# Weight narrowing with a mask made one piece ahead, combinations split where they are formed, and block sums accumulated in PSUM

## The chip, the core and the metric

The kernel runs on one core of one Trainium2 chip. The metric is the device time of one execution in microseconds (us). TensorE multiplies matrices into PSUM (eight banks of 2 KB per partition), VectorE, ScalarE and GpSimd work element by element, and SyncE issues most of the DMAs from one queue, in order. Every engine works through its own instructions in order; a wait holds up all that stands behind it.

## The reference, cut to what matters

```python
def _attn_ref(q, k, v, w_pre, w_post):            # batch 4, 12 heads, 448 tokens, 64
    scores = scale * np.matmul(q, k.transpose(0, 1, 3, 2))
    scores = np.einsum('bhij,hg->bgij', scores, w_pre)
    attn = softmax(scores)                        # written out in the original
    attn = np.einsum('bhij,hg->bgij', attn, w_post)
    return np.matmul(attn, v)
...
def _moe_ref(x, w_in, w_out, g_ln):               # 1792 x 768, inner width 1024
    h = x @ w_in
    solu = h * softmax(h)
    ln = (solu - mu) / np.sqrt(var + 1e-06) * g_ln
    return ln @ w_out
...
def _moe2_ref(x, w_in, w_out):                    # inner width 2048
    r = np.maximum(x @ w_in, 0.0)
    return (r * r) @ w_out
```

All weights of the two MLPs are float64 in DRAM, read as pairs of 32-bit words. The matrices are float32; each product is made of three matmuls of operands that are split into a high part and a remainder ("hi" and "lo").

## The kernel before

**Stages.** Attention, then the first MLP over 14 tiles of 128 tokens, then the second MLP in sixteen rounds. The order on each engine is the order of the code; nothing reorders it.

**Narrowing.** A float64 weight becomes a float32 by bit operations on its two words. `narrow` (line 75) takes a piece of 128x256: a Square on ScalarE of the high word read as a float32 (to see where the exponent is too small), then line 83 (shift the high word, mask it), line 87 (add the sign and top bit) and line 91 (add three bits of the low word) on VectorE. Values that are too small are then set to zero: by `flush` (lines 100 and 101) on GpSimd in the first MLP, by one more VectorE pass (line 96) in the second. The weights of the second MLP are 96 pieces, narrowed by the generator `w2stream`, of which the other code takes a step now and then (`steps2`). It holds three raw pieces (`nraw`), one `nsq` and two results (`nt`); SyncE loads the raw ones and stores the results to DRAM (w2iD, w2oD). About two thirds of the pieces fall into the first MLP, the rest into rounds 0 to 6.

**First MLP.** For tile m: `h1` (36 matmuls of 512 columns, line 459); the first part of `norm1` (maximum at line 712, exp at 715, the product at 718, bn_stats, and on GpSimd the power that gives rs); five steps of narrowing; `zt(m-1)` (eight transposes, line 747, with a cast on ScalarE and a subtraction on VectorE); the rest of the norm (nb at line 729 on VectorE, the scaling at 732 on ScalarE); five steps; the split of a later tile of x; and from tile 4 on two groups of `out1` (24 matmuls each, line 761, whose result ScalarE copies at line 769 into a tile that is stored to x2D), with seven steps behind each.

**Hand-over.** `prepare` runs beside the last nine output groups. The second MLP uses seven products (p1 to p7) instead of eight block products, so x and the weights are combined first. `mix_x` loads the four blocks of x (xb), combines them with four subtractions on VectorE (lines 890 to 894) and stores the results to DRAM (xtD); `load_xc` reads operands back (xr); `split_xc` (lines 925 and 926) splits them on ScalarE and VectorE. `mix_w` and `split_ti` do the same for weights, on GpSimd (lines 964 and 980) and ScalarE (line 979).

**Second MLP.** A round q takes 256 of the inner columns for half of the tokens (rounds 0 to 7, then 8 to 15). The list SEQ gives TensorE's order: the seven products (`prod`, nine matmuls of 448 columns each, line 1050) and, between them, seven output tiles of the round before (`y2`, twelve matmuls of 384 columns, line 1119, added on VectorE at line 1130). p1 and p2 share a bank, as do p5 and p3, and p7 and p4. `after` (line 1074) takes the sums off: u = p1 + p6, then u + p5, u + p5 + p7, u + p5 + p3 and u + p7 + p4, with a copy on ScalarE (line 1080) and five additions on VectorE (lines 1082 to 1096); `square` follows on ScalarE, and `lows` gives the remainder on VectorE (line 1063).

## Time and profile before

| | |
|---|---|
| time, median of 3 runs | 1254.18 us (1250.58 to 1259.58) |
| the profiled execution | 1259.37 us, of which the span of its instructions is 1257.6 us |
| busy in the span | TensorE 1083.1 us (86%), VectorE 738.3 (59%), GpSimd 699.9 (56%), ScalarE 585.0 (47%) |
| mean granted clock of TensorE | 0.940 of full speed |
| attention | 0 to 406 us |
| first MLP with the hand-over | 406 to 762.6 us |
| second MLP | 762.6 to 1257.6 us |

A busy share is an average over stages; what a stage is bound by is read from a stretch of its own. Times inside the span are us from its start. In a row of a timeline the engine's idle time ahead of the instruction stands in brackets, with what ended it. PE is TensorE, PEld its weight load, DVE VectorE, ACT ScalarE, POOL GpSimd, SPq the queue of SyncE.

### The profile page before, as it was taken

The page shows a single profiled execution, that of the slowest core. Times are in us where ns is not written, and L with a number is a line of the kernel's source. Part 1 is how long each engine was busy: PE and PEld are TensorE (multiplying, and loading weights), DVE is VectorE, ACT ScalarE, POOL GpSimd, SP SyncE. Part 2 cuts the span into 40 slices and gives each one's busy share as a digit, 9 for nine tenths or more (in the row PEclk, how much of TensorE's full clock was granted, in tenths as well). Part 3 has the DMA queues.
Part 4 walks back from the last instruction along what each step waited for, and adds up shares of the span by engine and source line. Part 5 has one row for each costly group of instructions (what it writes and reads, how often), then busy time and mean ns, then how long its engine had stood idle before and what let it go on. Part 6 is the DMA issues. An engine that isn't in the chain of part 4 may idle for free.

```text
span 1257.6 us, 31153 instructions
## 1 busy us (share of the span) xinstructions
PE 1083.1 (86%) x12488; PEld 908.4 (72%) x12488; DVE 738.3 (59%) x1293; ACT 585.0 (47%) x1212; POOL 699.9 (56%) x910
## 2 busy tenths in 40 slices
PE   8898979889898855898798666998889999999998
PEld 3555656556667644687687666888778899999998
DVE  3557768658662644555556455778877563344444
ACT  4666666668663322332332224643434556444432
POOL 3657988877755554453554353556654655555531
PEclk9899999989998977898999787999989999999999
DMA  6777887777664433343343485454443352222102
GB/s 178 207 219 221 236 249 219 234 219 209 203 194 121 147 105 112 114 143 97 115 142 107 141 289 163 125 175 142 143 142 106 117 179 99 66 73 63 51 26 88
DMA packets 131936, 187.91 MB, mean 149 GB/s; under 512 B 24752, under 2 KB 104368, under 8 KB 131792
## 3 DMA queue, kind: packets, MB, share of 16 engines
q1 hardware_dynamic: 122948, 161.40, 41.7%
q0 software_dynamic: 6464, 22.60, 6.6%
q10 hardware_dynamic: 2380, 1.93, 0.6%
q8 instruction: 98, 1.61, 0.6%
q14 instruction: 46, 0.38, 0.1%
HBM read 106.45 MB, written 40.89 MB: 117 GB/s over the span
## 4 chain that ended last, share of the span: by engine, by line
PE 20%; DVE 16%; DMA 11%; issue 7%; POOL 6%; ACT 5%; SPq 1%; POOLq 0%; DVEq 0%; ACTq 0%
PE ps_y L1119 11%; PE ps_h L1050 9%; DMA w2iD<-nt 3%; DVE nt L87 2%; POOL nt L101 2%; DMA w2oD<-nt 2%; POOL nsq L100 2%; DMA xr<-x2D 2%; DVE nt L91 2%; DVE y L1130 2%; DMA xr<-xtD 1%; DVE st L721 1%; DVE e L718 1%; DMA w1oraw<-w1oD 1%; DVE nt L83 1%
## 5 line engine op out<-in xcount | busy, mean ns | idle before, releaser
L1119 PE MATMUL ps_y<-to,gt 128*128 128x384 f32 x1332 | 250.9, 342 | 17.5 <-DVE y L1130 17.2
L1119 PEld LDWEIGHTS ps_y<-to,gt 128*128 128x128 f32 x1332 | 238.8, 192 | 24.0 <-DVE y L1130 18.2
L1050 PE MATMUL ps_h<-xc,ti 128*128 128x448 f32 x1008 | 222.4, 373 | 17.1 <-DVE h L1085 10.7
L1050 PEld LDWEIGHTS ps_h<-xc,ti 128*128 128x128 f32 x1008 | 192.0, 192 | 34.9 <-ACT ti L979 11.0
L761 PE MATMUL ps_o<-zt,w1o 128*128 128x384 f32 (+1 forms) x720 | 136.1, 351 | 30.7 <-ACT o L769 27.9
L761 PEld LDWEIGHTS ps_o<-zt,w1o 128*128 128x128 f32 x720 | 130.2, 209 | 35.3 <-ACT o L769 31.7
L299 PEld LDWEIGHTS ps_ring<-w,e 60*64 60x64 f32 (+1 forms) x5760 | 103.3, 138 | 72.1 <-issue 41.1
L318 DVE COPY at<-ps_ring 128x420 f32<-128x420 f32 x156 | 87.8, 610 | 108.5 <-PE ps_ring L299 108.4
L299 PE MATMUL ps_ring<-w,e 60*64 60x60 f32 (+2 forms) x5760 | 112.2, 222 | 31.8 <-issue 23.8
L80 ACT ACTIVATE nsq<-nraw 128x256 f32<-128x256 f32 x96 | 41.7, 434 | 210.0 <-POOL nt L101 145.6
L215 ACT COPY ssrc<-ps_ring 128x896 f32<-128x896 f32 x92 | 82.3, 906 | 107.3 <-PE ps_ring L208 94.0
L459 PE MATMUL ps_h<-w1i,xs 128*128 128x512 f32 x504 | 126.1, 409 | 3.8 <-POOL xs L702 3.4
L1130 DVE TENSOR_TENSOR y<-ps_y,y 128x768 f32<-128x768 f32 x97 | 92.1, 952 | 50.2 <-PE ps_y L1119 50.2
L260 ACT ACTIVATE e<-ps_pre,nm 128x448 f32<-128x448 f32 x180 | 113.1, 639 | 13.7 <-DVE nm L253 10.8
L459 PEld LDWEIGHTS ps_h<-w1i,xs 128*128 128x128 f32 x504 | 97.9, 196 | 27.7 <-POOL xs L702 4.3
L980 POOL TENSOR_TENSOR ti<-s,ti 128x384 fp32r<-128x384 f32 x64 | 69.6, 1099 | 74.1 <-ACT ti L979 72.5
L253 DVE TENSOR_REDUCE nm<-ps_pre 128x1 f32<-128x448 f32 x180 | 103.2, 611 | 12.4 <-PE ps_pre L242 12.4
L208 PE MATMUL ps_ring<-k,q 64*64 64x448 f32 x752 | 100.7, 558 | 5.6 <-ACT ssrc L215 3.7
L242 PE MATMUL ps_pre<-sdst,wpre_bd 64*64 64x448 f32 x720 | 100.5, 570 | 4.4 <-issue 2.7
L1063 DVE TENSOR_TENSOR gt<-h,gt 128x448 fp32r<-128x448 f32 x64 | 48.7, 761 | 92.0 <-ACT gt L1068 90.4
L338 PEld LDWEIGHTS ps_ring<-at,v 128*64 128x64 f32 x1536 | 77.7, 142 | 31.0 <-PE ps_pre L242 12.0
L83 DVE TENSOR_SCALAR nt<-nraw 128x256 uint32<-128x256 uint32 x96 | 39.3, 409 | 94.0 <-DMA w2iD<-nt 53.8
(112 smaller groups left out, 1660.0 us busy)
## 6 DMA issues: line engine op xcount, KB each, us to landing
sdst<-ssrc SPq DMA_DIRECT2D x166, 210.0 KB
nraw<-in_moe_w_in_dram SPq DMA_DIRECT2D x48, 256.0 KB
nraw<-in_moe_w_out_dram SPq DMA_DIRECT2D x48, 256.0 KB
ra<-w2iD SPq DMA_DIRECT2D x32, 384.0 KB
ro<-w2oD SPq DMA_DIRECT2D x32, 384.0 KB
w1raw<-in_moe_w_in_dram POOLq DMA_DIRECT2D x24, 256.0 KB, 6.3
w1raw<-in_moe_w_out_dram POOLq DMA_DIRECT2D x24, 256.0 KB, 5.7
w2iD<-nt SPq DMA_DIRECT2D x48, 128.0 KB
```

The source lines that it names most:

```text
L208: nc.tensor.matmul(out=ps[64 * u:64 * u + 64, e, 0:S], lhsT=qq[c][64 * e:64 * e + 64, p * n + u * half:p * n + u * half + 64], rhs=k[64 * ...
L215: (nc.vector.tensor_copy if dve else nc.scalar.copy)(ssrc[c][:, p:H:HP, :], ps[:, :, 0:S])
L242: nc.tensor.matmul(out=ps[b][64 * u:64 * u + 64, 0:S], lhsT=wpre_bd[64 * r:64 * r + m], rhs=ds[b][64 * r:64 * r + m], start=True, stop=True,)
L253: nc.vector.tensor_reduce(out=nm, in_=pres[s][b][:, 0:S], op=ALU.max, axis=AX.X, negate=True)
L260: nc.scalar.activation(out=e, in_=pres[s][b][:, 0:S], func=AF.Exp, bias=nms.pop((s, b)), scale=1.0, accum_out=sms[s][:, b:b + 1])
L299: nc.tensor.matmul(out=ps[64 * c:64 * c + 64, u, i0:i0 + ng * RH], lhsT=e[64 * u:64 * u + m, o:o + 64], rhs=w[64 * u:64 * u + m, b, g0:g0 ...
L318: nc.vector.tensor_copy(dst[:, 1:3] if u else dst[:, 0:4:3], pv)
L459: nc.tensor.matmul(out=ps[:, u], lhsT=t[:, a, cc], rhs=w1i[cc][:, w, u * 512:(u + 1) * 512], start=(cc == 0 and a == 0 and w == 0), stop=( ...
L761: nc.tensor.matmul(out=ps[:, 0:width], lhsT=w1o[k][:, w, cc * 128:(cc + 1) * 128], rhs=zT[:, a, k, 0:width], start=(k == 0 and i == 0), st ...
L1050: nc.tensor.matmul(out=bank[b][:, 0:HT], lhsT=t[:, w, c], rhs=xc[name][:, a, c], start=(first and c == 0 and i == 0), stop=(c == HC - 1 an ...
L1119: nc.tensor.matmul(out=ps[:, u - u2[0], 0:DM // 2], lhsT=gt[:, a, f, o:o + 128], rhs=w[:, v, f, u * (DM // 2):(u + 1) * (DM // 2)], start= ...
L1130: nc.vector.tensor_tensor(out=yo, in0=po, in1=yo, op=ALU.add)
```

## The change

The change has four parts.

1. *Narrowing.* ScalarE writes its Square straight into the piece's result tile, and one GpSimd instruction turns it into a mask there (0, or the word 0x3FFFFFFF). Both are issued one piece ahead. VectorE then makes three passes, each from the raw words and the tile itself. Lines 96 and 101 have no successor. The pieces of the first MLP (60 of 96) have five raw and five result tiles; the other 36 have three and three, in another pool.
2. *First MLP.* The rest of the norm moves behind the first output group; the steps become 3, 3, 4 and 4 per tile. The tiles through which x and the output weights are loaded come from another pool.
3. *Hand-over.* p1, p5, p7 and p6 of the first half are split directly from the blocks in which they are formed; only p4's operand goes through DRAM. The second half of x is combined as before, on GpSimd, and its operands are loaded two ahead.
4. *Block sums.* ScalarE copies p1 into the bank in which p6 then accumulates, and that sum into the bank in which p5 and later p3 accumulate. Three additions on VectorE become three more copies on ScalarE. SEQ puts one output tile between p1 and p6 and between p6 and p5.

```diff
+    def w2stream(todo, pool, nr, nt):
...
+        def mask(i):
+            if i in todo:
+                t = ts[i] = pool.tile([128, WP], F32, tag="nt", name="nt", bufs=nt)
+                nc.scalar.activation(out=t, in_=words(i)[1].bitcast(F32), func=AF.Square)
+                nc.gpsimd.tensor_scalar(
+                    out=t, in0=t, scalar1=2.0**-30, scalar2=2.0 - 2.0**-23, op0=ALU.is_ge, op1=ALU.mult
+                )
...
+        for i in range(nr - 1):
+            load(a + i)
+        mask(a)
+        for i in todo:
+            load(i + nr - 1)
+            mask(i + 1)
+            low, high = words(i)
+            bits = ts[i].bitcast(U32)
+            stt = nc.vector.scalar_tensor_tensor
+            stt(out=bits, in0=high, scalar=3, in1=bits, op0=ALU.logical_shift_left, op1=ALU.bitwise_and)
+            yield True
+            if ready:
+                store()
+            stt(out=bits, in0=high, scalar=0xC0000000, in1=bits, op0=ALU.bitwise_and, op1=ALU.bitwise_or)
+            yield True
+            stt(out=bits, in0=low, scalar=29, in1=bits, op0=ALU.logical_shift_right, op1=ALU.bitwise_or)
...
+    stream = w2stream(range(FIRST), m1b_p, 5, 5)
...
         next(norm)
-        steps2(5)
+        steps2(3)
         if m > 0:
             zt(m - 1)
-        run(norm)
-        steps2(5)
+        steps2(3)
...
-        for _ in range(2):
+        for i in range(2):
             if outs:
                 out1(*outs.pop(0))
-            steps2(7 if m else 0)
+            steps2(4 if m else 2)
+            if i == 0:
+                run(norm)
+    run(stream)
...
     def prepare():
         load_ra(0)
-        load_xc(0, "p1")
-        mx = mix_x(0, nc.vector)
...
+        parts = [load_xb(0, 0), load_xb(0, 1)]
...
+            b11, b12, b21, b22 = qs = parts[c]
+            split_xc(0, "p1", c, b11)
+            yield True
+            mix_x(qs, 0, nc.vector)
+            mix_x(qs, 1, nc.vector)
+            split_xc(0, "p5", c, b11)
+            yield True
+            mix_x(qs, 2, nc.vector)
+            mix_x(qs, 3, nc.vector)
+            split_xc(0, "p7", c, b12)
+            yield True
+            split_xc(0, "p6", c, b22)
+            store_xt(0, c, "p4", b21)
...
         if name == "p1":
+            nc.scalar.copy(bank["W"][:, 0:HT], ps)
+        elif name == "p6":
+            nc.scalar.copy(bank["Y"][:, 0:HT], ps)
             us[q] = m2_p.tile([128, HT], F32, tag="u", name="u", bufs=1)
             nc.scalar.copy(us[q], ps)
-        elif name == "p6":
-            add(out=us[q], in0=ps, in1=us[q], op=ALU.add)
         elif name == "p5":
             hs[q] = height()
-            add(out=hs[q], in0=ps, in1=us[q], op=ALU.add)
+            nc.scalar.copy(hs[q], ps)
         elif name == "p7":
             add(out=hs[q], in0=ps, in1=hs[q], op=ALU.add)
         elif name == "p3":
-            h = height()
-            add(out=h, in0=ps, in1=us[q], op=ALU.add)
-            square(h, 0, 1)
+            square(height(), 0, 1, ps)
...
-    SEQ = ["p1", "p6", 4, "p5", 5, "p7", 6, 3, 0, "p3", 1, 2, "p2", "p4"]
+    SEQ = ["p1", 4, "p6", 5, "p5", 6, "p7", 3, 0, "p3", 1, 2, "p2", "p4"]
...
-                steps2(2 if q else 1)
+                steps2(2 if q and k < 10 else 1)
```

*ScalarE, a tile of the first MLP.* From the exp to the copies of the two output groups (xs is the split of x, o1 an output group); before:

```order
L715 ACTIVATE e_8257,sm_8258<-ps_h_8218,nm_8255 128x1024
L80 ACTIVATE nsq_8279<-nraw_8206 128x256
L749 CAST zt_8098<-ps_tr_8282 128x4x128
L749 CAST zt_8098<-ps_tr_8289 128x4x128
L732 ACTIVATE e_8257<-e_8257,nb_8296,rs_8268 128x1024
L80 ACTIVATE nsq_8307<-nraw_8272 128x256
L701 CAST xs_8310<-xraw_8216 128x768
L769 COPY o1_8338<-ps_o_8313 128x384
L80 ACTIVATE nsq_8349<-nraw_8300 128x256
L769 COPY o1_8382<-ps_o_8357 128x384
```

and of the change:

```order
L714 ACTIVATE e_8225,sm_8226<-ps_h_8186,nm_8223 128x1024
L799 ACTIVATE nt_8241<-nraw_8095 128x256
L748 CAST zt_8077<-ps_tr_8248 128x4x128
L748 CAST zt_8077<-ps_tr_8255 128x4x128
L799 ACTIVATE nt_8264<-nraw_8135 128x256
L700 CAST xs_8271<-xraw_8184 128x768
L768 COPY o1_8299<-ps_o_8274 128x384
L799 ACTIVATE nt_8304<-nraw_8175 128x256
L799 ACTIVATE nt_8313<-nraw_8239 128x256
L731 ACTIVATE e_8225<-e_8225,nb_8317,rs_8236 128x1024
L768 COPY o1_8345<-ps_o_8320 128x384
```

The Squares now write nt, and the norm's scaling (e from nb and rs) has moved from behind the casts of zt to behind the first output copy.

*ScalarE, the hand-over.* Casts of x operands (xc) and weights (ti) and the output copies, in round 0's preparation; before:

```order
L925 CAST xc_9942<-xr_9916 128x448
L925 CAST xc_9942<-xr_9918 128x448
L925 CAST xc_9942<-xr_9920 128x448
L769 COPY o1_9978<-ps_o_9953 128x384
L979 CAST ti_9981<-ra_9912 128x384
L979 CAST ti_9986<-s_9940 128x384
L979 CAST ti_9991<-s_9938 128x384
L769 COPY o1_10023<-ps_o_9998 128x384
L979 CAST ti_10026<-s_9949 128x384
L979 CAST ti_10037<-s_9951 128x384
L979 CAST ti_10042<-ra_9914 128x384
```

and of the change:

```order
L955 CAST xc_9764<-xb_9740 128x448
L955 CAST xc_9769<-xb_9740 128x448
L768 COPY o1_9797<-ps_o_9772 128x384
L955 CAST xc_9802<-xb_9742 128x448
L955 CAST xc_9805<-xb_9746 128x448
L1009 CAST ti_9817<-ra_9736 128x384
L1009 CAST ti_9820<-s_9758 128x384
L768 COPY o1_9848<-ps_o_9823 128x384
L955 CAST xc_9764<-xb_9748 128x448
L955 CAST xc_9769<-xb_9748 128x448
L955 CAST xc_9802<-xb_9750 128x448
L768 COPY o1_9886<-ps_o_9861 128x384
```

The casts now read the blocks xb; four operands are begun side by side where one was (its next three came behind loads, as xr).

*ScalarE, a round of the second MLP,* from the end of p4's squares into the next round (gt is the squared result, ps_h2 the bank of p1); before:

```order
L1068 CAST gt_10317<-h_11106 128x448
L979 CAST ti_11112<-ra_10812 128x384
L80 ACTIVATE nsq_11119<-nraw_11011 128x256
L1080 COPY u_11136<-ps_h2_11126 128x448
L80 ACTIVATE nsq_11152<-nraw_11075 128x256
L979 CAST ti_11212<-ra_11115 128x384
L80 ACTIVATE nsq_11215<-nraw_11124 128x256
```

and of the change:

```order
L1103 CAST gt_10108<-h_10954 128x448
L1009 CAST ti_10960<-ra_10641 128x384
L1114 COPY ps_bW_10109<-ps_h2_10969 128x448
L799 ACTIVATE nt_10983<-nraw_10939 128x256
L1116 COPY ps_bY_10111<-ps_bW_10109 128x448
L1118 COPY u_11014<-ps_bW_10109 128x448
L799 ACTIVATE nt_11018<-nraw_10981 128x256
L799 ACTIVATE nt_11057<-nraw_11016 128x256
L1121 COPY h_11070<-ps_bY_10111 128x448
```

Where u was one copy of p1, p1 now goes to bank W, W to bank Y and to u, and Y to h, with Squares of the narrowing between.

## Rows read from the trace of the kernel before

**Rows 1.** Windows: us; busy (x count) of PE, PEld, DVE, ACT, POOL; PEclk; DMA.

```profile
433.20:458.30 25.10, 9.96 (x44) 7.44 (x44) 15.84 (x25) 7.70 (x14) 14.74 (x15) 0.84 0.42 126
...
535.43:554.62 19.19, 18.00 (x92) 16.08 (x93) 12.11 (x25) 6.75 (x14) 9.84 (x12) 1.00 0.45 144
688.70:718.00 29.30, 17.60 (x81) 17.25 (x82) 14.81 (x32) 8.49 (x18) 13.93 (x18) 0.71 0.38 122
718.00:762.60 44.60, 33.86 (x226) 33.34 (x225) 22.24 (x26) 13.65 (x31) 15.78 (x12) 0.85 0.77 256
762.60:795.70 33.10, 20.37 (x84) 17.79 (x82) 21.74 (x28) 16.75 (x33) 15.99 (x13) 0.79 0.50 158
```

**Rows 2.** Timeline, TensorE, first MLP: start us, us, instructions [idle before <-releaser].

```profile
418.01 1.09 PE L747 MATMUL ps_tr<-id_sb,e 128*128 128x128 f32 x8 [0.17 <-ACT e L732]
...
561.09 4.45 PE L761 MATMUL ps_o<-zt,w1o 128*128 128x384 f32 x24 [0.79 <-ACT o L769]
565.38 8.59 PE L459 MATMUL ps_h<-w1i,xs 128*128 128x512 f32 x36
...
711.42 6.69 PE L761 MATMUL ps_o<-zt,w1o 128*128 128x384 f32 x24 [11.67 <-ACT o L769]
```

**Rows 3.** Timeline, all engines, tiles 2 to 4 of the first MLP.

```profile
446.06 1.22 DVE L712 TENSOR_REDUCE nm<-ps_h 128x1 f32<-128x1024 f32 x1
...
454.69 0.43 ACT L80 ACTIVATE nsq<-nraw 128x256 f32<-128x256 f32 x1 [6.12 <-POOL nt L101]
...
456.84 0.15 DVE L729 SCALAR_TENSOR_TENSOR nb<-mv,rs 128x1 f32<-128x1 f32 x1
...
457.02 1.24 ACT L732 ACTIVATE e<-e,nb,rs 128x1024 f32<-128x1024 f32 x1 [0.94 <-DVE nb L729]
...
469.05 0.55 DVE L83 TENSOR_SCALAR nt<-nraw 128x256 uint32<-128x256 uint32 x1 [7.52 <-DMA w2oD<-nt]
```

**Rows 4.** Timeline: a VectorE pass beside a GpSimd instruction, two places.

```profile
579.67 1.86 POOL L702 TENSOR_TENSOR xs<-xraw,xs 128x768 fp32r<-128x768 f32 x1 [2.52 <-ACT xs L701]
579.85 1.96 DVE L91 SCALAR_TENSOR_TENSOR nt<-nraw,nt 128x256 uint32<-128x256 uint32 x1
...
715.83 1.00 POOL L100 TENSOR_SCALAR nsq<-nsq 128x256 f32<-128x256 f32 x1 [0.56 <-ACT nsq L80]
716.16 0.50 DVE L91 SCALAR_TENSOR_TENSOR nt<-nraw,nt 128x256 uint32<-128x256 uint32 x1
```

**Rows 5.** Timeline, hand-over and round 0 of the second MLP.

```profile
728.61 1.43 DVE L890 TENSOR_TENSOR xb<-xb 128x448 f32<-128x448 f32 x1
...
741.88 0.62 DVE L893 TENSOR_TENSOR xb<-xb 128x448 f32<-128x448 f32 x1
...
750.27 0.56 ACT L925 CAST xc<-xr 128x448 fp32r<-128x448 f32 x1 [13.15 <-DMA xr<-xtD]
...
751.16 11.59 PE L761 MATMUL ps_o<-zt,w1o 128*128 128x256 f32 x72 [10.62 <-ACT o L769]
...
780.87 7.48 PE L1050 MATMUL ps_h<-xc,ti 128*128 128x448 f32 x27 [10.70 <-DVE h L1085]
```

**Rows 6.** Windows, single rounds of the second MLP; columns as in rows 1.

```profile
856.42:890.75 34.33, 29.95 (x148) 27.78 (x147) 27.52 (x41) 13.83 (x28) 17.98 (x15) 0.95 0.62 195
922.57:962.77 40.20, 32.37 (x148) 30.30 (x147) 30.91 (x41) 14.89 (x30) 20.75 (x17) 0.87 0.41 133
1049.36:1076.88 27.52, 27.52 (x149) 26.46 (x148) 6.03 (x10) 18.02 (x32) 14.76 (x14) 1.00 0.26 86
```

**Rows 7.** Round from 856.42, VectorE: line group (busy, mean ns | idle); window of tile nt.

```profile
L87 DVE SCALAR_TENSOR_TENSOR nt<-nraw,nt 128x256 uint32<-128x256 uint32 x6 | 5.7, 950 | 0.1
...
856.42:890.75 34.33, 15.82 (x24) 0.95 0.62 195
```

**Rows 8.** Timeline, a settled round.

```profile
1097.06 7.50 PE L1050 MATMUL ps_h<-xc,ti 128*128 128x448 f32 x36
...
1104.20 0.52 ACT L1080 COPY u<-ps_h 128x448 f32<-128x448 f32 x1
```

More of the change, by code (lines that the diff above doesn't have):

```diff
@@ L791, in store @@
         def store():
-            i, t = ready.pop(0)
+            i = ready.pop(0)
             src, dst, k, o = w2pieces[i]
-            nc.sync.dma_start(out=dst[k * 128:(k + 1) * 128, o:o + WP], in_=t)
+            nc.sync.dma_start(out=dst[k * 128:(k + 1) * 128, o:o + WP], in_=ts.pop(i))
             narrowed.append(i)
-        load(0)
-        load(1)
-        for i in range(len(w2pieces)):
-            sq = nar_p.tile([128, WP], F32, tag="nsq", name="nsq", bufs=1)
-            t = nar_p.tile([128, WP], F32, tag="nt", name="nt", bufs=2)
-            eng = nc.gpsimd if in_first else nc.vector
-            for step, _ in enumerate(narrow(raws[i], sq, t, eng)):
-                if step == 1:
-                    load(i + 2)
-                if step == 2 and ready:
-                    store()
-                yield True
-            if eng is nc.gpsimd:
-                flush(sq, t)
+        a = todo[0]
@@ new lines, in load_xb, with mix_x @@
+        qs = []
+        for k in range(2):
+            for t in range(2):
+                b = wi2_p.tile([128, HT], F32, tag=f"xb{k}{t}", name="xb", bufs=2)
+                r0 = (k * HC + c) * 128
+                nc.sync.dma_start(out=b, in_=x2D[r0:r0 + 128, t0 + t * HT:t0 + (t + 1) * HT])
+                qs.append(b)
+        return qs
+    def mix_x(qs, i, eng):
+        b11, b12, b21, b22 = qs
+        out, x, y = ((b11, b12, b11), (b12, b22, b12), (b22, b22, b11), (b21, b21, b22))[i]
+        eng.tensor_tensor(out=out, in0=x, in1=y, op=ALU.subtract)
@@ L906, in load_xc @@
         for c in range(HC):
[L907 removed]
+            if p and ORDER.index(name) % 2:
+                r = wi2_p.tile([128, HT], F32, tag=f"xb{c // 2}{c % 2}", name="xr", bufs=2)
+            else:
+                r = wi2_p.tile([128, HT], F32, tag="xr", name="xr", bufs=3)
             if name in ("p1", "p2", "p3"):
```

119 lines of the change are left out of this document (56 added, 63 removed).

## Prediction

> **What bounds the kernel now.** I read the profile from the outside in. The page says 86% busy for TensorE, an average over three stages with different limits. So I took the timeline of TensorE alone and cut the span at its waits: attention to 406 us (the change leaves it alone), the first MLP with its hand-over to 762.6, then sixteen rounds q of the second MLP. Rounds 9 to 15 last 27.52 us with TensorE busy for all of it [rows 6]: they are at their floor. The waits are in the middle.
>
> In the first MLP the reader is to see that tiles of equal work differ. A tile late in the stage (36 matmuls of line 459, 8.4 us; two groups of 24 of line 761, 4.25 us each; 1.0 us of transposes [rows 2]) is 17.9 us of TensorE, and the best one takes 19.2 [rows 1]; the first ones hold only 9.4 us of work and take 25.1 [rows 1]. From the transposes of tile 0 (418.0) to those of tile 13 (718.0) it is 300 us, for 3x9.4 + 9x17.9 + 13.8 = 203 us of matmuls. What ends last there is the norm's chain, and it waits on the narrowing of weights that is interleaved with it: the maximum of the tile starts at 446.06, the nb of line 729 only at 456.84, because a Square of the narrowing had waited 6.12 us for GpSimd's line 101 (one buffer nsq) with the casts of line 749 behind it on ScalarE [rows 3]. On VectorE line 83 waits up to 7.5 us for the store of an earlier piece (two buffers nt) [rows 3], with the next tile's maximum behind it. At the end of the stage the same chain costs 11.67 us at 711 [rows 2], in a stretch at granted clock 0.71 [rows 1], so more than half of it at the lower of the two levels (1.2 against 2.4 GHz).
>
> In the hand-over ScalarE waits 13.15 us for tiles that were combined, written to DRAM and read back; its copy of line 769 stands behind, and TensorE waits 10.62 us. In round 0 it waits another 10.70 us for an addition on VectorE [rows 5]. In rounds 1 to 8 (795.7 to 1049.36, 253.7 us against 8x27.52 = 220.2) VectorE is busy 27.5 of 34.3 us in one round and 30.9 of 40.2 in the worst [rows 6].
>
> **First MLP.** A piece was Square, three VectorE passes and two GpSimd passes, in series over one nsq and two nt. Now it is Square and one GpSimd pass, issued a piece ahead, then three VectorE passes, over five nt and five nraw. A tile issues 14 steps of three to a piece (4.7 pieces) instead of 24 steps of five (4.8). So the work is the same, the series is gone, and a store has some three pieces of time to land before ScalarE needs its buffer. The wait for the store moves from VectorE to ScalarE, where the norm's exp, the casts and the output copies stand behind it; with five buffers I cost it at nothing, and if the cover went it would be the 7.5 us of [rows 3] at most, per tile.
>
> VectorE per tile: it was busy 12.1 us of the 19.2 us tile [rows 1], and stays there. ScalarE is at 6.8 and GpSimd at 9.8 of 19.2 [rows 1], with one GpSimd pass per piece less. None reaches 17.9, so tiles 4 to 12 become TensorE's: 17.9 plus half of the 1.2 us gap that the best tile shows (18.0 busy of 19.2), 18.5 us each. Moving the nb and ScalarE's line 732 behind the first output group delays the norm by ten VectorE passes (at most 0.5 us each where nothing holds them [rows 4]) and an output copy; it has the 17.9 us to the next transposes, and needs about 13. Tiles 1 to 3 have no output group as cover: chain of about 13 us plus GpSimd passes that hold VectorE (below), 15 us each. The last tile has three groups as cover: 15. Sum 45 + 9x18.5 + 15 = 226.5 instead of 300: **-73**. Bounds: 203 us (-97), and half of the waits staying (-48).
>
> **A rule against it.** Every VectorE pass of the new narrowing reads two SBUF tiles, and the mask is one more kind of work on GpSimd. What the rows show: with GpSimd's 1.86 us tensor_tensor running, the same pass of line 91 lasted 1.96 us; inside a 1.00 us GpSimd tensor_scalar it lasted 0.50 and ended before it [rows 4]. The Trainium skill, "SBUF — State Buffer", section "Who interferes with whom", says that a VectorE instruction with two SBUF inputs and a GpSimd one that reads SBUF exclude each other for the whole instruction. The trace agrees for the tensor_tensor and not for the tensor_scalar, which is the mask's form. By the rule each of 36 late masks could hold VectorE for up to the mask's own length, an estimate of 36 us in all; by the rows it is about 0.1 each. I take the rows and keep the other as a rival.
>
> **Hand-over.** Four of the seven operands of round 0 are now split from the tiles in which they are formed; twelve stores of combinations become three, and the twelve loads of p1, p6, p5 and p7 go from SyncE's queue. No cast waits for a read-back. VectorE has 12 combinations and 12 subtractions; one takes 0.62 us alone and 1.43 beside GpSimd [rows 5], so 15 to 34 us in all, and I take 24 since GpSimd works for part of it. They begin when the first loads have landed, some 7 us after the transposes of tile 13 as now: 31 us. TensorE has three groups of 4.25 us and six narrower ones there, between 2.8 (two thirds of 4.25) and 3.9 us (72 matmuls in 11.59 [rows 5]): 30 to 36 us. Where the two alternate, I take 35 instead of the 44.6 from 718.0 to 762.6 [rows 1]: **-10** (bounds -14 and +4: an output copy still stands behind these casts on ScalarE).
>
> **Round 0** took 33.1 us [rows 1]. The 10.70 us wait falls, but three operands still come by load, each behind the split of the one before; each of the new copies into PSUM now stands behind such casts. I take 30: **-3** (bounds -12, +4).
>
> **Rounds 1 to 8.** VectorE loses three additions per round and the gating pass, and gets 8 pieces of three passes instead of about 6 of four. In the round from 856.42, its 27.5 us hold 15.8 of narrowing (24 passes) [rows 6, 7]; the rest less three additions of 0.6 is 9.9. With 24 passes between 0.50 [rows 4] and the 0.95 us that line 87 has in that round [rows 7], nearest to the latter since GpSimd keeps its tensor_tensors: 24x0.88 = 21, so 31 us of VectorE, 33 with its waits. The pieces then last through round 4 and not into round 6. Rounds: 28.5, 3x33, 2x27.6, 2x28.5 = 240 instead of 253.7: **-14** (bounds -33 at the floor, +10 if VectorE needs 36).
>
> **Three copies on ScalarE instead of three additions.** The trace has no PSUM-to-PSUM copy; the nearest is the same 448 columns from PSUM to SBUF, 0.52 us [rows 8], less than any wait discussed here. p6 now needs p1's copy, with only one output tile (12 matmuls, 2.1 us) between. In a settled round p1 is the third quarter of 36 matmuls from 1097.06, so it ends at 1102.7; the copy begins at 1104.20, behind ScalarE's work on p4 [rows 8], and ends at 1104.72. p6 could begin at 1104.75. So the copy arrives just in time; a tenth of a microsecond per round, **+1**. The cover is thin: any further microsecond on ScalarE ahead of it is paid in full. Bounds 0 and +16.
>
> **Sum.** -73 - 10 - 3 - 14 + 1 = -99. The profiled execution took 1259.4 us, which gives 1160. It lies 5 above the median of 1254.2, from which the sum would be 1155. I put 1158.
>
> **Rivals.**
> 1. *The norm's chain stays the bound.* The mask stands in GpSimd's order behind the tile's rs (which waits for VectorE) and the splits, and VectorE's first pass waits for it. For it: GpSimd is busiest in the early tiles, 14.7 of 25.1 us [rows 1]. Against: one piece ahead, and five buffers. With half of the waits left, -48 there and -70 in all: about 1190.
> 2. *VectorE and GpSimd bound rounds 1 to 5.* If the masks exclude VectorE's passes, or in-order waits between them add up, rounds 2 to 4 go to 40 us as the worst does now: +21 against my sum, 1180.
> 3. *All covers hold:* rounds 1 to 8 at the floor, the first MLP near 210 us: 1158 - 19 - 16 = about 1125.
> 4. *Slower than before.* p6 and p5 wait each time for ScalarE, which waits for a store behind SP's loads. It decides only where sixteen rounds pay over 99/16 = 6.2 us each, the longest wait of a Square in [rows 3]; at 8 us a round, 1158 + 128 = 1286. The settled rounds have no narrowing, so half of them can't pay it.
> 5. *No gain in the first MLP,* were its tiles bound by something else that the trace doesn't show: -26 in all, 1230.
>
> **How the numbers follow.** Forecast 0.55, rival 1 0.17, rival 2 0.12, rival 3 0.10, rival 4 0.02, rival 5 0.04. The predicted time is the forecast's, 1158. The range 1125 to 1192 takes in rivals 1 to 3 and leaves out 4, 5 and some of each edge. One per cent (12.5 us) is about what a measurement of this kernel can tell from no change: faster by more than that holds in all but rival 4 and the worse part of 5, 0.96; within it 0.02; slower 0.02.
>
> **What would show it.** Tiles 4 to 12 of the first MLP at 18 to 19 us with the granted clock near 1.0 and no wait over 1 us ahead of the transposes; no 10 us wait before the last output groups; no load of xtD in the hand-over but p4's; in the settled rounds TensorE at 27.5 to 27.7 us, with the wait before p6 on ScalarE under 0.3 us. I am wrong if tiles stay above 20 us (then the chain had another cause), if rounds 2 to 4 exceed 36 us, or if TensorE waits over 1 us per settled round for the copies.

## The result

The changed kernel takes 1209.4 us (median; 1208.2 to 1211.9) against 1254.6 us before in the same session: a ratio of 0.964 (95% interval 0.960 to 0.968). It is faster, but by 45 us where 96 were predicted. The profiled execution's span went from 1257.6 to 1208.8 us, and the stages account for all of it. Boundaries are starts of TensorE's groups, as in the prediction; zt(m) are the transposes of tile m, a round ends where the next round's first output tile starts. Before the change p1 and p6 of the next round stand ahead of that tile, after it p1 alone, so 2.0 us of matmuls (p6) moved from round 0 to the rest: like for like, round 0 is 38.0 us and the rest hardly moved.

| stretch | before, us | after, us | predicted, us |
|---|---|---|---|
| end of attention to zt(0) | 11.3 | 21.5 | no change |
| zt(0) to zt(4), four tiles | 96.5 | 80.0 | (-73 us over zt(0) to zt(13)) |
| zt(4) to zt(13), nine tiles | 203.5 | 154.1 | |
| hand-over | 44.6 | 35.9 | 35 |
| round 0 | 33.1 | 36.0 | 30 |
| rounds 1 to 8 | 253.7 | 263.2 | 240 |
| six settled rounds | 165.1 | 166.4 | 165.7 |
| the rest | 43.1 | 45.0 | no change |

The first stretch, attention, ended at 406.7 and 406.8 us. These are the page's first lines for the kernel after:

```profile
span 1208.8 us, 30990 instructions
...
PE 1067.8 (88%) x12490; PEld 898.9 (74%) x12490; DVE 701.6 (58%) x1214; ACT 602.5 (50%) x1260; POOL 709.7 (59%) x876
...
PEclk9889999998999967899999978989999999999999
```

The windows of the kernel after have the columns of [rows 1]: us, busy time of PE, PEld, DVE, ACT and POOL, granted clock, DMA.

```profile
428.20:508.20 80.00, 54.47 (x225) 45.98 (x226) 51.33 (x97) 28.36 (x51) 47.03 (x39) 0.79 0.43 134
508.20:662.20 154.00, 154.00 (x817) 140.63 (x816) 108.41 (x204) 55.90 (x107) 65.50 (x62) 1.00 0.44 135
...
698.20:734.20 36.00, 19.10 (x74) 16.20 (x73) 19.63 (x27) 17.83 (x37) 18.97 (x16) 0.74 0.50 171
...
801.83:839.62 37.79, 31.55 (x149) 28.57 (x148) 27.61 (x38) 16.18 (x33) 31.20 (x26) 0.91 0.53 174
...
909.69:937.40 27.71, 27.71 (x148) 26.39 (x147) 10.84 (x13) 13.13 (x26) 14.65 (x13) 1.00 0.18 57
```

The second line is the gain: from tile 4 on TensorE is busy for all of the 154 us at full granted clock, a tile every 17.58 us (the last 13.4), where the best tile before took 19.19 [rows 1]. The first line is the largest hole: TensorE works 54 of 80 us. Round 0 and the round from 801.83 are the others; the latter has GpSimd busy 31.2 us, where a like round before had 18.0, and VectorE 27.6 as there [rows 6]. The last line is a round without narrowing, at its floor.

### The profile page after: what moved, and what is told of

The parts are those of the page before. It is cut to its first block, busy times and chain, and to the rows that moved or that the text cites. A ratio compares the mean times of both kernels' runs of the same rounds, so it can differ in the third digit from the quotient of the medians.

```text
span 1208.8 us, 30990 instructions
## 1 busy us (share of the span) xinstructions
PE 1067.8 (88%) x12490; PEld 898.9 (74%) x12490; DVE 701.6 (58%) x1214; ACT 602.5 (50%) x1260; POOL 709.7 (59%) x876
## 4 chain that ended last, share of the span: by engine, by line
PE 65%; DMA 9%; POOL 7%; issue 7%; DVE 6%; ACT 5%; SPq 1%; ACTq 0%; POOLq 0%; DVEq 0%
PE ps_y L1153 14%; PE ps_o L760 9%; PE ps_h L457 7%; PE ps_ring L297 6%; PE ps_h L1085 6%; PE ps_ring L336 6%; PE ps_ring L206 5%; PE ps_pre L240 5%; PE ps_bY L1085 4%; DMA sdst<-ssrc 3%; POOL nt L800 3%; PE ps_bW L1085 2%; POOL ti L1010 1%; DMA w1oraw<-w1oD 1%; DMA w2iD<-nt 1%
## 5 line engine op out<-in xcount | busy, mean ns | idle before, releaser
L1153 PE MATMUL ps_y<-to,gt 128*128 128x384 f32 x1332 | 249.6, 339 | 13.7 <-POOL to L1018 11.6
L1153 PEld LDWEIGHTS ps_y<-to,gt 128*128 128x128 f32 x1332 | 237.2, 191 | 19.6 <-POOL to L1018 12.6
L800 POOL TENSOR_SCALAR nt<-nt 128x256 f32<-128x256 f32 x96 | 112.7, 1174 | 69.9 <-ACT nt L799 63.5
L1085 PE MATMUL ps_h<-xc,ti 128*128 128x448 f32 x576 | 125.5, 371 | 4.8 <-ACT h L1101 4.8
L760 PE MATMUL ps_o<-zt,w1o 128*128 128x384 f32 (+1 forms) x720 | 123.6, 331 | 2.8 <-ACT o L768 2.8
L760 PEld LDWEIGHTS ps_o<-zt,w1o 128*128 128x128 f32 x720 | 120.1, 193 | 3.3 <-ACT o L768 3.3
L258 ACT ACTIVATE e<-ps_pre,nm 128x448 f32<-128x448 f32 x180 | 113.3, 640 | 17.7 <-DVE nm L251 14.8
L1085 PEld LDWEIGHTS ps_h<-xc,ti 128*128 128x128 f32 x576 | 109.3, 191 | 14.3 <-ACT h L1101 5.2
L206 PE MATMUL ps_ring<-k,q 64*64 64x448 f32 x752 | 103.2, 564 | 6.6 <-ACT ssrc L213 3.2
L1098 DVE TENSOR_TENSOR gt<-h,gt 128x448 fp32r<-128x448 f32 x64 | 59.4, 928 | 84.4 <-ACT gt L1103 84.4
L820 DVE SCALAR_TENSOR_TENSOR nt<-nraw,nt 128x256 uint32<-128x256 uint32 x96 | 53.2, 554 | 71.9 <-POOL nt L800 65.9
```

The source lines that it names most:

```text
L206: nc.tensor.matmul(out=ps[64 * u:64 * u + 64, e, 0:S], lhsT=qq[c][64 * e:64 * e + 64, p * n + u * half:p * n + u * half + 64], rhs=k[64 * ...
L258: nc.scalar.activation(out=e, in_=pres[s][b][:, 0:S], func=AF.Exp, bias=nms.pop((s, b)), scale=1.0, accum_out=sms[s][:, b:b + 1])
L760: nc.tensor.matmul(out=ps[:, 0:width], lhsT=w1o[k][:, w, cc * 128:(cc + 1) * 128], rhs=zT[:, a, k, 0:width], start=(k == 0 and i == 0), st ...
L800: nc.gpsimd.tensor_scalar(out=t, in0=t, scalar1=2.0**-30, scalar2=2.0 - 2.0**-23, op0=ALU.is_ge, op1=ALU.mult)
L1085: nc.tensor.matmul(out=bank[b][:, 0:HT], lhsT=t[:, w, c], rhs=xc[name][:, a, c], start=(first and c == 0 and i == 0), stop=(c == HC - 1 an ...
L1153: nc.tensor.matmul(out=ps[:, u - u2[0], 0:DM // 2], lhsT=gt[:, a, f, o:o + 128], rhs=w[:, v, f, u * (DM // 2):(u + 1) * (DM // 2)], start= ...
```

## Experiments

In the tables "start" is the time from the end of attention to zt(4) and "9 tiles" that from zt(4) to zt(13). The end of attention itself, whose code is the same in all, lay between 400.3 and 411.8 us in the profiled executions, so stretches are compared, not spans.

### The early tiles

TensorE's timeline of the kernel after shows what is missing in the first four tiles:

```profile
428.22 1.97 PE L746 MATMUL ps_tr<-id_sb,e 128*128 128x128 f32 x8 [10.31 <-ACT e L731]
...
470.92 1.97 PE L746 MATMUL ps_tr<-id_sb,e 128*128 128x128 f32 x8 [11.25 <-ACT e L731]
```

Each wait, in brackets, is for the scaling of e (line 731), which the change put behind the casts of the output weights. On ScalarE these casts wait up to 10.7 us for their load. The obvious theory is this order on ScalarE; one run undid it alone:

```diff
         steps2(3)
+        if m < GT + 1:
+            run(norm)
```

> Only in tiles 0 to 3 of the first MLP the rest of the norm (nb and ScalarE's scaling of e) is put back ahead of the casts of x and of the output weights. Theory A (ScalarE's casts of w1oraw, each waiting 7.1 to 10.7 us for a load, hold the scaling of e back): the wait of zt(0) to zt(3) for e (10.3, 8.9, 11.3 and 5.3 us) falls below 3 us each, zt(0) starts near 418 instead of 428, zt(4) near 487 instead of 508, the whole near 1188 us (1183 to 1195). Rival theory (the mask and VectorE's first pass behind it set the pace of these tiles, whatever the order on ScalarE): zt(0) comes up to 10 us earlier, but the distances to zt(4) stay 17 to 23 us; 1199 us or more.

The median is 1213.9 us (0.965 of before; 0.960 to 0.970). zt(0) came 6.3 us earlier after attention, but the next distances were 20.2, 20.8, 21.2 and 25.3 us, and zt(4) gained nothing: theory A falls. The timeline of this run (ScalarE, GpSimd, VectorE, between zt(1) and zt(2)) shows the circle:

```profile
446.96 0.83 ACT L686 CAST w1o<-w1oraw 128x768 fp32r<-128x768 f32 x1 [0.94 <-DMA w1oraw<-w1oD]
...
446.10 3.65 POOL L687 TENSOR_TENSOR w1o<-w1oraw,w1o 128x768 fp32r<-128x768 f32 x2 [1.06 <-ACT w1o L686]
449.83 2.46 POOL L800 TENSOR_SCALAR nt<-nt 128x256 f32<-128x256 f32 x2
...
450.94 0.43 DVE L820 SCALAR_TENSOR_TENSOR nt<-nraw,nt 128x256 uint32<-128x256 uint32 x1 [7.75 <-POOL nt L800]
...
452.27 1.22 DVE L711 TENSOR_REDUCE nm<-ps_h 128x1 f32<-128x1024 f32 x1
```

The next tile's maximum (line 711) stands on VectorE behind a narrowing pass (line 820); this waits for its mask on GpSimd (line 800); the mask stands behind the subtractions of the output weights (line 687), and these behind casts that wait for a load. Two runs test it. One moves the casts and subtractions to the end of the tile, behind its narrowing steps, with the norm early as above:

```diff
-        for kk in sorted(wr):
-            split_w1_out(kk, wr.pop(kk))
...
             if i == 0:
                 run(norm)
+        for kk in sorted(wr):
+            split_w1_out(kk, wr.pop(kk))
```

> The rest of the norm stands early as in the run before, and the casts and subtractions of the output weights, with their loads where they were, are put at the end of the tile, behind its narrowing steps. Theory E (a circle: the next norm's first reduction on VectorE stands behind a narrowing pass, which waits 7.8 to 8.2 us for its mask, which GpSimd makes after 3.7 us of w1o subtractions, which wait for a load that SyncE sends late): the 7.8 to 8.2 us waits of VectorE fall under 3 us, tiles 0 to 3 come 17 to 18.5 us apart, zt(4) stands near 492 instead of 508: 1190 to 1197 us. Rival (the tile's chain from the reduction to the scaled e is itself 20 us long): distances stay at 20 us, 1205 us or more.

The median is 1195.8 us (0.949; 0.944 to 0.953). Tiles 0 to 3 came 14.8, 16.2 and 16.9 us apart, and 24.5 to zt(4), where the last weights are now late for `out1` (waits of 2.44 and 0.99 us); the start fell from 101.4 to 87.5 us. The weights moved without the norm early was not run. The other moves the mask alone:

```diff
-                nc.gpsimd.tensor_scalar(
+                nc.vector.tensor_scalar(
```

> The mask's one instruction is given to VectorE instead of GpSimd, in both parts of the narrowing, and nothing else. Theory D (GpSimd is what is short: its 1.17 us mask stands behind 3.6 us of w1o subtractions in tiles 0 to 3, and in rounds 1 to 5 it is busy 25 to 31 us of 33 to 38): tiles 0 to 3 come 17 to 18.5 us apart instead of 20.0 on average, rounds 1 to 5 sum to 160 us or less instead of 175.6, the waits for the split of to (11.6 us in all) go: 1180 to 1193 us. Rival (ScalarE's queue is what is short: casts of w1o waiting for loads in tiles 0 to 3, Square waiting for the store of nt in the rounds; the mask only shows it): both stretches stay within 4 us of the changed kernel's, 1203 to 1215 us.

It took 1240.3 us (0.985; 0.982 to 0.988), slower than the changed kernel in both stretches (start 113.6, rounds 1 to 8 278.6 us), which neither theory had. A line of VectorE's waits over this whole execution (us in all, times, longest; 31.1 us of it lie before zt(4), 34.5 in rounds 1 to 8), a line of TensorE's in rounds 1 to 8, and a window of the round to be set beside that from 801.83:

```profile
DVE nt L800 <- ACT nt L799: 85.6, 35, 7.0
```

```profile
PE ps_y L1153 <- DVE y L1164: 17.9, 6, 6.5
```

```profile
823.90:867.70 43.80, 32.65 (x148) 30.33 (x148) 29.68 (x45) 16.06 (x33) 21.66 (x19) 0.84 0.48 150
```

GpSimd is relieved, 21.7 instead of 31.2 us, and the round is 6 us longer. In rounds 1 to 8 of the changed kernel TensorE waited 11.6 us for a split on GpSimd and 1.7 for the output tiles' additions on VectorE; now the first are gone and the second are 17.9, since these additions stand behind masks that wait for ScalarE's Square. So GpSimd's load is one of the things that TensorE waited for, but taking the mask off it only hands the wait on; what comes late in both kernels is the Square.

### Round 0

Here p5 waited 11.47 us for the copy into bank Y. The timeline of the kernel after (ScalarE, then TensorE):

```profile
711.47 0.43 ACT L799 ACTIVATE nt<-nraw 128x256 f32<-128x256 f32 x1 [6.30 <-DMA nraw<-in_moe_w_in_dram]
...
713.84 0.52 ACT L1116 COPY ps_bY<-ps_bW 128x448 f32<-128x448 f32 x1
...
714.41 3.73 PE L1085 MATMUL ps_bY<-xc,ti 128*128 128x448 f32 x9 [11.47 <-ACT ps_bY L1116]
...
720.08 2.02 PE L1085 MATMUL ps_bY<-xc,ti 128*128 128x448 f32 x9
```

The copy of 0.52 us stands behind a Square that waits for the second stream's first load. The wait costs twice: the nine matmuls after it take 3.73 us, those of a later product 2.02, and the granted clock of the round is 0.74, so part of it at the lower level (1.2 against 2.4 GHz). The first of the two runs here narrows 72 pieces in the first MLP and takes one step at each place of the rounds; the second also leaves round 0 without narrowing:

```diff
-    FIRST = 60
+    FIRST = 72
...
-            steps2(4 if m else 2)
+            steps2((4 if m < 4 else 6) if m else 2)
...
-                steps2(2 if q and k < 10 else 1)
+                steps2(1)
--- second run, besides
-            if p == 0:
+            if p == 0 and q:
```

> 72 instead of 60 of the 96 pieces are narrowed in the first MLP (six instead of four steps twice in each tile from the fifth on), and one step instead of two at each place of the rounds after, so that 24 pieces are spread over rounds 0 to 5. Theory D (narrowing is what loads GpSimd and ScalarE in rounds 1 to 5, and tiles 4 to 12 of the first MLP, at 17.6 us each, are bound by TensorE and have room): tiles 4 to 12 stay within 1 us of 17.6, rounds 1 to 7 sum to 235 to 245 us less 27.7 for the last instead of 235.5: the whole 1180 to 1192 us. Rival (TensorE's rounds wait for the copies into PSUM and late splits whatever the narrowing): rounds gain under 6 us, 1203 us or more. Second rival (GpSimd has no room in the first MLP): tiles 4 to 12 grow to over 19 us and give back the gain.

> As the run with 72 pieces in the first MLP, but no narrowing step in round 0; the 24 pieces are spread over rounds 1 to 6. Theory F (round 0 lost 11.5 us at its third product because ScalarE's copy into Y stands behind a Square that waits 6.3 us for the first load of the second stream): the wait falls to 5 us or less, round 0 takes 29 to 32 instead of 36.4 us: 1188 to 1193 us. Rival (the copy waits for the casts of the next operand, whose loads are late by themselves): the wait stays above 8 us, round 0 at 35 us or more, 1195 us or more.

The first gave 1196.5 us (0.952; 0.947 to 0.956): nine tiles stay at 154.1 us, rounds 1 to 8 take 248.4, round 0 36.4; the time is a little above theory D's range. The second gave 1193.5 us (0.947; 0.943 to 0.950), with round 0 at 29.4, but the wait of p5 only fell to 9.4: the copy still stands behind casts of operands, one of which waited 5.9 us for its load. Both theories have a part: the narrowing cost 7 us of the round, the late operands hold the rest. Rounds 1 to 8, with the narrowing of round 0 moved into them, gave 4 us back (252.4), so the two runs are not told apart as a whole. Nor is the copy itself what makes the round late: in the run with the sums on VectorE (below), which has no copy into PSUM, TensorE's wait in round 0 is for an addition, and the round takes 38.2 us without p6:

```profile
721.18 7.40 PE L1085 MATMUL ps_h<-xc,ti 128*128 128x448 f32 x27 [16.51 <-DVE h L1120]
```

### Rounds 1 to 8

A chain of the kernel after (SyncE, ScalarE, TensorE, near 810 us):

```profile
801.16 6.90 SPq L974 DMA_DIRECT2D ro<-w2oD  x2
...
811.87 0.48 SPq L807 DMA_DIRECT2D w2oD<-nt  x1
...
816.14 0.43 ACT L799 ACTIVATE nt<-nraw 128x256 f32<-128x256 f32 x1 [6.90 <-DMA w2oD<-nt]
816.47 0.53 ACT L1116 COPY ps_bY<-ps_bW 128x448 f32<-128x448 f32 x1
...
817.05 2.12 PE L1085 MATMUL ps_bY<-xc,ti 128*128 128x448 f32 x9 [1.37 <-ACT ps_bY L1116]
```

SyncE stands 6.90 us at loads of ro, whose tile a split on GpSimd still holds, and 3.23 at loads of ra; the store of nt goes behind; Square waits for its buffer; the copy into Y stands behind Square, and p5 behind the copy. TensorE's waits in rounds 1 to 8 sum to 27 us, 11.6 of them for the split "to" on GpSimd (us in all, times, longest; the last line is the kernel before, where VectorE's additions of output tiles were 16.8 of 21.5 us):

```profile
PE ps_y L1153 <- POOL to L1018: 11.6, 3, 4.3
PE ps_bY L1085 <- ACT ps_bY L1116: 10.3, 5, 4.5
PE ps_bW L1085 <- ACT ps_bW L1114: 3.4, 3, 2.6
PE ps_y L1153 <- DVE y L1164: 1.7, 3, 0.6
```

```profile
PE ps_y L1119 <- DVE y L1130: 16.8, 12, 5.0
```

So the change did take VectorE out of TensorE's way here (16.8 to 1.7 us), and waits for ScalarE's copies and GpSimd's split took its place.

Three runs work on single links of that chain: the loads of ro issued in the next round, five buffers nt (from one buffer h), and the store right behind its third pass.

```diff
             split_to(q, 1)
-            load_ro(n)
...
+        if k == 2 and q:
+            load_ro(q)
--- second run
-        return m2_p.tile([128, HT], F32, tag="h", name="h", bufs=3)
+        return m2_p.tile([128, HT], F32, tag="h", name="h", bufs=2)
-    in_second = w2stream(range(FIRST, len(w2pieces)), wi2_p, 3, 3)
+    in_second = w2stream(range(FIRST, len(w2pieces)), wi2_p, 3, 5)
--- third run
-            if ready:
-                store()
...
             ready.append(i)
+            store()
```

> Only the loads of the second layer's output weights for the next round (ro) are issued at the third step of that round, when the GpSimd subtraction that frees their tile is over, instead of at the twelfth step of the round before, where SyncE's queue stood at them for 6.9 to 11.4 us with the stores of nt behind. Theory C (Square waits for nt because its store is queued behind ro): ScalarE's waits at Square for nt stores fall from 47 us to under 20, rounds 2 to 5 get 2 to 5 us shorter each: 1190 to 1201 us. Rival (GpSimd's late masks bound the narrowing, the store comes from a late piece anyway): less than 4 us, 1205 to 1212 us.

> The second stream has five buffers nt instead of three; the room comes from one of the three buffers h of the block sums. Theory G (the ring of three nt is what holds the rounds: Square of a piece waits for the store of the piece three before, SyncE sends that store late, and ScalarE's copies into PSUM and casts stand behind Square): Square's waits for stores fall from 45 us to under 15 us between 734 and 970 us, rounds 1 to 5 sum to 155 to 163 us instead of 175.6: 1189 to 1198 us; settled rounds stay at 27.7 us, as two buffers h are enough. Theory D2 (GpSimd's work, 25 to 31 us a round, is what holds them, through the late split of to): Square waits less, but the rounds keep their waits for to (11.6 us) and sum to 170 us or more: 1203 us or more.

> A piece's store is issued right behind its third pass instead of two steps later, in both streams, and nothing else. Theory G (ring of nt): Square waits less by about two steps of the narrowing, 2 to 3 us at each of the 14 waits in the rounds: rounds 1 to 5 sum to 160 to 168 us, 1194 to 1202 us. Rival (SyncE then stands at each store for VectorE, and the loads of ro, ra and nraw behind it come later): rounds 1 to 5 sum to 175 us or more, 1207 us or more, and tiles 0 to 3 of the first MLP may lose too.

None helps: 1218.7 us (0.969; 0.965 to 0.974), 1208.7 (0.960; 0.956 to 0.965) and 1218.8 (0.967; 0.962 to 0.972), with rounds 1 to 8 at 267.6, 260.3 and 264.2 us. The first is above the ranges of theory and rival, the other two are in their rivals'. With five buffers the waits of Square for stores are gone, and it waits for raw loads in their place; this is ScalarE in that run, 734 to 960 us:

```profile
ACT nt L799 <- DMA nraw<-in_moe_w_out_dram: 22.4, 11, 2.9
ACT nt L799 <- DMA nraw<-in_moe_w_in_dram: 18.8, 9, 4.9
```

With the loads of ro later, SyncE stood at those of ra instead, and Square's waits for stores grew from 45 to 56 us. Loads and stores stand in one queue of SyncE, and in these runs a freed buffer only changed the name of the wait. What does change the rounds is how much narrowing they hold, and where the block sums are made. The block sums as before, alone:

```diff
-            nc.scalar.copy(bank["W"][:, 0:HT], ps)
-        elif name == "p6":
-            nc.scalar.copy(bank["Y"][:, 0:HT], ps)
...
+        elif name == "p6":
+            add(out=us[q], in0=ps, in1=us[q], op=ALU.add)
...
-    SEQ = ["p1", 4, "p6", 5, "p5", 6, "p7", 3, 0, "p3", 1, 2, "p2", "p4"]
+    SEQ = ["p1", "p6", 4, "p5", 5, "p7", 6, 3, 0, "p3", 1, 2, "p2", "p4"]
```

> Everything as changed, but the block sums and the order of products as in the kernel before: one copy on ScalarE, four adds on VectorE, no copies into PSUM, and the products that open and close a round take the old order. Theory B1 (the copies into PSUM put TensorE behind ScalarE, whose Square waits for buffers nt, so this part costs time while narrowing lasts): rounds 0 to 5 lose the waits of ps_bY and ps_bW (11.5 us in round 0, about 13 us in rounds 1 to 7): 1185 to 1200 us. Theory B2 (GpSimd's masks and splits bound these rounds, TensorE would wait for other things instead): 1205 to 1213 us. Prediction's own theory (the adds are what cost time in rounds 1 to 5): 1215 us or more.

1209.2 us (0.961; 0.957 to 0.965), the same as with them: rounds 1 to 8 are 6.6 us shorter, round 0 is 4.2 longer (2.0 of them since p6 now lies in it). It is theory B2's range, and what TensorE waits for in rounds 1 to 8 shows why: not for the copies any more, but for VectorE's additions, as in the kernel before:

```profile
PE ps_y L1154 <- DVE y L1165: 16.0, 10, 4.2
```

And the sums in PSUM alone, put into the kernel before:

> The kernel before with the block sums in PSUM alone: the two copies into PSUM and the copy of p5 on ScalarE, the new order of products, the two seeding products; narrowing, hand-over and weights as before. Prediction's own theory (four adds of 0.62 us less a round on VectorE, which is busy 26 to 31 us in rounds 2 to 5, shorten these): rounds 1 to 8 sum to 240 to 248 us instead of 253.7, 1241 to 1250 us. Theory B1 (each copy puts ScalarE's queue between two products of TensorE): rounds 1 to 8 sum to 253 us or more, 1254 us or more, settled rounds 27.7 us.

1259.3 us against 1257.7 (1.000; 0.997 to 1.004), rounds 1 to 8 at 251.6: no gain there either (the edit takes three additions from a round, not four). TensorE's waits in these rounds, to be set beside the 16.8 us for VectorE before:

```profile
PE ps_bW L1050 <- ACT ps_bW L1079: 14.2, 6, 3.2
PE ps_bY L1050 <- ACT ps_bY L1081: 3.6, 2, 3.2
PE ps_y L1118 <- DVE y L1129: 1.6, 3, 1.0
```

The next runs join what had helped: weights split late, 72 pieces, none in round 0. Then 84 pieces, 21 steps a tile in the first MLP and one step at every second place of rounds 1 to 6. Both then with the block sums of before, and last five buffers nt.

> Three edits of the runs before together: the output weights split at the end of a tile with the norm early, 72 pieces in the first MLP, no narrowing in round 0. If what each showed is independent, the profiled spans add: 1208.8 less 14.9 and less 15.8, that is 1178 us (1173 to 1184). If they stand in each other's way (tiles 0 to 3 become shorter and less narrowing is hidden there, or the later start of the second stream makes rounds 1 to 6 longer): 1187 us or more.

> As the joined run, with 84 of the 96 pieces in the first MLP (21 steps in each tile from the fifth on) and 12 spread over rounds 1 to 6, one step at every second place. Theory H (in rounds 1 to 6 the narrowing as such, on whichever engine stands at it, costs TensorE's time: 72 left 24 pieces and an excess of 24 us over six settled rounds of 27.7): the excess halves to 8 to 15 us and tiles 4 to 12 stay at 17.6 us: profiled span 1157 to 1164 us. Rival 1 (the excess comes from the second half's operands and the splits on GpSimd, not from the narrowing): 1168 us or more with tiles still at 17.6. Rival 2 (the first MLP has no room for 2 more pieces in a tile, 12.0 of 17.1 us being busy on VectorE there): tiles 4 to 12 grow past 18.5 us and give the gain back.

> The run with 84 pieces, with the block sums and product order of the kernel before (one copy on ScalarE, four adds on VectorE). Theory B2 (the block sums in PSUM neither gain nor cost much: with 36 pieces left for the rounds both ways took the same): within 5 us of the run with 84 pieces, settled rounds 27.5 instead of 27.7 us, round 0 longer by 3 to 5. Theory B1 (with little narrowing left, the copies into PSUM are what still makes TensorE wait, 20 us at ps_bW and ps_bY in the joined run): 6 us or more faster. Prediction's own theory (the adds are dearer): 6 us or more slower.

> The joined run (72 pieces in the first MLP, 24 over rounds 1 to 6, no narrowing in round 0, output weights split late) with the block sums and product order of the kernel before. Theory B1 (with the narrowing spread thin, the copies into PSUM on ScalarE are what keeps rounds 1 to 7 at 28.9 to 34.4 us; VectorE has room for four adds): rounds 1 to 6 at 27.5 to 29.5 us, round 0 near 33, settled rounds 27.5: 1150 to 1160 us. Rival (24 pieces are too many for VectorE beside the adds, as rounds of 34 to 38 us with 36 pieces showed): rounds 1 to 6 at 31 us or more: 1167 us or more.

> The run with 72 pieces and the sums on VectorE, with five buffers nt and two buffers h. Theory G (two rounds of 35.3 and 32.3 us are left there, because Square waits up to 9.7 us for a store of nt that SyncE sends behind the loads of ro): these two rounds fall to 29.5 us or less and the sum of rounds 1 to 6 from 180.4 to 166 to 173: 1153 us median less or about (1148 to 1157), profiled span 1146 to 1153. Rival (the wait moves on to the loads of nraw, which stand in the same queue behind the same ro, as with 60 pieces): rounds 1 to 6 sum to 177 us or more, 1160 us or more.

| kernel | median, us | ratio to before (95%) | start | 9 tiles | round 0 | rounds 1 to 8 |
|---|---|---|---|---|---|---|
| after | 1209.4 | 0.964 (0.960 to 0.968) | 101.4 | 154.1 | 36.0 | 263.2 |
| three joined, 72 pieces | 1175.0 | 0.934 (0.927 to 0.940) | 87.4 | 154.3 | 28.3 | 251.1 |
| 84 pieces | 1180.9 | 0.937 (0.932 to 0.942) | 87.6 | 168.7 | 28.8 | 240.8 |
| 84, sums on VectorE | 1164.9 | 0.924 (0.918 to 0.930) | 87.5 | 168.9 | 33.1 | 224.1 |
| 72, sums on VectorE | 1164.0 | 0.925 (0.920 to 0.930) | 86.1 | 154.3 | 32.0 | 237.6 |
| the same, five nt | 1156.5 | 0.919 (0.916 to 0.923) | 87.6 | 154.3 | 32.0 | 235.0 |

The joined run is at the sum that was expected. In rounds 1 to 8 two effects stand apart. With 32, 24 and 12 pieces narrowed in them (of the 36 that the changed kernel leaves, four fall into round 0) they take 263, 251 and 241 us with the sums in PSUM, and 257, 238 and 224 with those on VectorE (floors 222 and 220): a piece costs 0.9 to 2.5 us, and the copies into PSUM, with the order of products that goes with them, 7, 13 and 17 us in all, more the less narrowing there is beside them: with 84 pieces the whole is 16 us faster without them, as theory B1 has it, where B2 held with 60. With 12 pieces and the sums on VectorE a round with narrowing is at its floor (a window of that kernel, columns as above):

```profile
764.73:792.25 27.52, 27.52 (x148) 26.46 (x147) 18.80 (x22) 11.43 (x23) 21.93 (x19) 1.00 0.42 136
```

while with the copies such a round still waits for ScalarE, as TensorE's timeline of the kernel with 84 pieces shows:

```profile
725.23 2.77 PE L1087 MATMUL ps_bW<-xc,ti 128*128 128x448 f32 x9 [1.94 <-ACT ps_bW L1116]
...
732.35 2.14 PE L1087 MATMUL ps_bY<-xc,ti 128*128 128x448 f32 x9 [1.36 <-ACT ps_bY L1118]
```

Rival 2 of the run with 84 pieces came true as well: at 21 steps a tile takes 19.6 us, 14.4 us more over the nine, and that is more than the rounds gained (10.3). With the sums on VectorE, 72 pieces missed both of their ranges (rounds 1 to 6 at 30 us each). Five buffers did little for the rounds once more (235.0 against 237.6; rounds 1 to 6 sum to 177.9, the rival's figure): Square waits 36 us for raw loads, where it waited 35 for stores. The last kernel is 53 us under the changed one; its interval overlaps those of the two kernels above it, so which of the three is best is not shown. What stays open is SyncE's queue: that it is what makes Square late is read from the rows and from three edits that moved the wait without removing it; no run took its loads to another queue.

## Why the prediction was off

**Right.** The direction; tiles 4 to 12 as TensorE's own (18.5 us put; 17.58 found in all but the first of them, since the gap of the best tile closed altogether, and 20.0 in the first, from zt(3) to zt(4)); the last tile (15 put, 13.4 found); the hand-over (35 put, 35.9 found, no wait over 2.3 us ahead of its output groups); the settled rounds (a tenth of a microsecond each put, two tenths found, a copy of 0.53 us).

**The start, 25 us short** (tiles 4 to 13 gave 7 of them back). The step that failed is "Tiles 1 to 3 have no output group as cover: chain of about 13 us plus GpSimd passes": 15 us each were put, 20.0 found, and zt(0), taken as unmoved, came 10 us later. The 15 us was the right length of the chain: it is what the run with the late weights shows (14.8 to 16.9). The step counted engines' work and left out the casts and subtractions of the output weights, which exist only in these tiles and which the move put ahead of the scaling on ScalarE and which already stood ahead of the masks on GpSimd. It is the first rival's mechanism, the mask behind splits on GpSimd, with loads ahead of these splits that the rival didn't name. (Its own sum has a slip: -48 and the other terms make -74, so about 1185.)

**Round 0, 6 us short** (8 like for like). The prediction saw that the copies stand behind casts, but costed it inside 30 us; it missed that the second stream starts here with empty buffers, so that Square waits for a first load with casts and the copy behind. Narrowing in this round cost 7 us; the late operand loads, which the prediction named, hold p5 another 9.4 us without it.

**Rounds 1 to 8, 23 us short.** The failed step is that VectorE sets these rounds after the change too. It was put at 31 us in a 33 us round and found at 27.6 in one of 37.8, and TensorE's waits for it fell from 16.8 to 1.7 us: the relief came, but the rounds got longer, as two terms that the sum had at next to nothing took its place. The first is the copies. Square's place in ScalarE's order, ahead of them, was costed at nothing with five buffers ("if the cover went it would be the 7.5 us"), but the second stream has three, and found waits reach 7.2 us. The copies were put at +1 from a settled round; TensorE waited 13.7 us for them, and they cost 7 to 17 us in the rounds with narrowing, up to the upper bound of 16 us that the prediction gave them and a little past it.

The second is GpSimd, whose masks in these rounds stand in no term: it was busy 31.2 us where a like round before had 18.0, and its split "to" held TensorE 11.6 us, waits that went when the mask was taken off it (and fell to 1.1 us with the sums on VectorE, where TensorE waited for its additions). The prediction's own sign of being wrong came: rounds 3 and 4 took 37.8 and 36.9 us, over 36.

The second rival's price (+21 us) was about right, though by another mechanism. The fourth rival's mechanism was there, but only in the rounds with narrowing, which is why it didn't decide. Why Square itself is late, SyncE's queue or the engines that hold the tiles of its loads, stays open.

**The rule on shared ports.** VectorE beside GpSimd behaves as the rows of before said. The timeline of the kernel after (GpSimd, VectorE):

```profile
458.29 2.47 POOL L800 TENSOR_SCALAR nt<-nt 128x256 f32<-128x256 f32 x2
460.84 2.04 POOL L701 TENSOR_TENSOR xs<-xraw,xs 128x768 fp32r<-128x768 f32 x1
...
459.86 0.50 DVE L824 SCALAR_TENSOR_TENSOR nt<-nraw,nt 128x256 uint32<-128x256 uint32 x1
...
461.26 1.91 DVE L824 SCALAR_TENSOR_TENSOR nt<-nraw,nt 128x256 uint32<-128x256 uint32 x1
```

Inside two masks the pass takes 0.50 us, beside the tensor_tensor 1.91. It is so throughout this trace: all 59 narrowing passes that begin inside a GpSimd tensor_tensor of over 0.8 us end 0.28 to 0.33 us behind its end, whereas the 57 that lie inside a mask take 0.41 to 0.66 us. The Trainium skill, "SBUF — State Buffer", section "Who interferes with whom", has a VectorE instruction with two SBUF inputs contend with any GpSimd instruction that reads SBUF and doesn't tell these forms apart; the trace agrees for the tensor_tensor alone, and the estimate of 36 us by the rule was rightly left out of the sum.

## What to carry to other kernels

When work is moved off a busy engine, follow the queue of the engine that receives it: a 0.5 us copy behind an instruction that waits for a DMA costs what the DMA costs. Work that exists only in the first iterations of a stage needs its own sum there. An engine that stops being waited for isn't yet time gained: ask which engine got its work and who waits for that one. And where freeing one buffer only renames the wait, take work out of the stretch, or put it where the bound engine has room, up to the point where that stretch grows itself (18 steps a tile cost nothing here, 21 cost 2 us a tile).
